# Layer norm blocks turned through three lent PSUM banks, later exponentials, and the memory's key sums on GpSimd

## The chip, the cores and the metric

The kernel runs on one core of one Trainium2 chip. Its engines are TensorE (PE, with its weight loads as PEld), VectorE (DVE), ScalarE (ACT), GpSimd (POOL) and SyncE (SP), which issues most DMAs. PSUM holds eight banks of 128 partitions by 512 fp32 values; TensorE writes there, ACT and DVE read it. The metric is the device time of one execution in microseconds (us), as the median of several runs; lower is better. Before the change the median of three runs is 2346.03 us (2342.25 to 2346.14).

## What is computed

A pre-norm transformer block on 2048 tokens of width 1024: layer norm, a memory-augmented attention of 32 heads of 32 (Infini-attention, four segments of 512 tokens), residual, a second layer norm, a GELU MLP of width 3584, residual. All in fp32. The part that the change touches is this, for each of the four segments `s`:

```python
phi = lambda t: jnp.where(t > 0, t + 1.0, jnp.exp(t))
logits = q_s @ k_s.T * scale + mask          # causal variant over the segment
a_dot  = softmax(logits) @ v_s
pq  = phi(q_s)
num = pq @ M                                  # memory of earlier segments
den = pq @ z + 1e-6                           # its key sums
o   = g * num / den + (1 - g) * a_dot
pk = phi(k_s)
M = M + pk.T @ v_s
z = z + pk.sum(over tokens)
```

`x` goes through `_layernorm` (mean and variance over the width, eps 1e-5) before the projections to q, k and v.

## The kernel before

Every fp32 matrix product is made of three passes in a rounded type: an operand is split into a high half (`yh`, `kh`, `pth`, ...: a cast, mostly on ACT) and a low half (`yl`, `kl`, `ptl`, ...: a subtraction, mostly on DVE), and `mm3` adds high by high, high by low and low by high in PSUM.

The tokens are worked in two halves of 1024, each of two segments (`sl` 0 and 1, so `s = 2 * half + sl`). A half has these stages: attention, output projection (`wo_first`, `wo_second`), second layer norm, the MLP's first product (class `Mixer`), and after the second half the MLP's second product (class `Second`) for all tokens.

**Attention.** The loop goes over eight groups `g` of four heads, inside it over the two segments. One pass is a unit, made by `dense(g, sl, ws, u)`: eight chunks of key projection into a bank `kps`, eight of query projection into `qps`, eight of value projection into `vps`, with a `yield` after each chunk. At each yield one of the six steps of a head of the unit before runs (`heads`, `slot`, the string `PLAN`): scores `pqk`, softmax (`pr`, `mx`, `nm`), transposes `ppt` of the probabilities with their halves `pth` and `ptl`, and products `po` with the values. 24 chunks of a unit thus lie beside the 24 steps of four heads.

After the keys are projected, `kh` (L408, ACT) and `kl` (L414, DVE) are the halves of `kps`; DMAs stack them into `ks`. `phi_parts` (L356) makes exp and relu of the same bank on ACT (`e` L358, `r` L359), named before `kl`; `phi_sum` (L364, DVE, two chunks later) adds them to `pk` and leaves the sum over the tokens in the column `zc`. With the queries it goes the same way: `qh` L422, `e`, `r`, `ql` L429, `pq`. Keys need phi in segments 0 to 2, queries in segments 1 to 3.

What is left of a unit (`late`, L461) runs inside the next one: value transposes `vn`, memory reads `pm` (`memory`, L472), the update `pmm` of the memory (`update`, L489) and the transposes `pom`. Their small matmuls are queued (`smalls`, `one_small`) and put singly between the transposes and products of the heads. The memory stands in `MZ`: for each group 128 columns of `M` (four blocks of 32 by 32 on the diagonal) and four columns of key sums. `update` writes the key sums: ACT spreads `zc` over four columns by the head mask `hsel`, into columns 128 to 131 of the bank of `pmm` (L491), and DVE adds them to `MZ` (L495), after four DVE adds of the blocks (L494). The next segment of the same group casts `MZ` to `mzh` (L441, DVE) and `mzl` (L442, POOL).

**PSUM.** The eight banks are named by tags: `d` has three (`ps_dense`: `kps`, `qps`, `vps`, `pkn`, `vn`, `pm`, `pmm`, `pom` in turn), `qk` two (`pqk`), `pt` two (`ppt`), `av` one (`po`). A tile takes a bank of its tag when the last reader of an earlier tile there is done.

**Layer norm before the projections.** `ln1(half, sl)` takes four tiles of 128 tokens: statistics on DVE, three small POOL instructions (L132, L133, L138) for scale `v` and offset `nb`, the scaling on ACT (`xt`, L167), then for each half of the width four transposes into one bank (L146, PE), the cast `yh` (L148, ACT) and the difference `yl` (L150, DVE). The bank comes from `take`: always the one of `av`. Segment 1 of each half is normalised inside the first unit of that half (`interleave(d, ln1(half, 1, ...))`), when no heads run yet; segment 0 of the second half inside the last nine pairs of the mixer's first half. Segment 0 of the first half has its own code (`opening`), which the change leaves alone.

**Order.** From the mixer to the end of a half, and in the opening, each engine keeps the order of the program (`in_order`). In the attention the framework's scheduler orders each engine's queue at build time, by program order and its own estimate of when inputs are ready; on the chip each queue then runs in that order.

Of the kernel before, what the change touches and what calls it, by code (L numbers as in the profile page):

```python
# [9 lines left out]
F32 = mybir.dt.float32  # L10
# [32 lines left out]
def build(tc, x, wq, wk, wv, wo, beta, w1, b1, w2, b2, out):  # L43
# [9 lines left out]
    ident = const.tile([P, P], F32, name="ident")  # L53
    make_identity(nc, ident)
    sel = const.tile([P, 76], F32, name="sel")
    hsel, gcol = sel[:, 0:4], sel[:, 8:8 + NG]
    nc.vector.memset(hsel, 0.0)
    for j in range(4):
        nc.vector.memset(hsel[32 * j:32 * j + 32, j:j + 1], 1.0)
    mhalf = const.tile([P, 1], F32, name="mhalf")  # L60
# [138 lines left out]
    def ln1(half, sl, delay=0, aside=None):  # L199
        xs = []  # L200
        for t in range(4):
            xt = lnp.tile([P, D], F32, tag="ln", name="xt", bufs=4)
            r0 = half * HT + (4 * sl + t) * P
            nc.sync.dma_start(xt, x[0, r0:r0 + P, :])
            xs.append(xt)
        for _ in range(delay):
            yield
        acts["y", sl] = yh, yl = seg_tiles(sl, "y")

        def take(name):  # L210
            return psum.tile([P, 512], F32, tag="av", name=name, bufs=1)

        yield from ln_tiles(lnp, xs, yh, yl, False, act=True, aside=aside,
                            fold=lambda src, t4: ln_transpose(lnp, src, yh, yl, t4, take))
# [125 lines left out]
    def attention(half, first):  # L340
# [15 lines left out]
        def phi_parts(ps):  # L356
            e, r = tmp("e"), tmp("r")
            nc.scalar.activation(e, ps, AF.Exp)  # L358
            nc.scalar.activation(r, ps, AF.Relu)  # L359
            return e, r  # L360
# [36 lines left out]
        def dense(g, sl, ws, u):  # L397
            s = 2 * half + sl
            behind = acts.pop("late", iter(()))
            kps = ws.pop("kps", None)  # L400
            if kps is None:
                kps = ps_dense("kps")
                for c in project(ws["k"], sl, "kps", kps):
                    if c >= 2:
                        next(behind, None)
                    yield
            kh, kl = tmpr("kh"), tmpr("kl")
            nc.scalar.copy(kh, kps)  # L408
            if s < 3:
                kparts = phi_parts(kps)  # L410
            qps = ps_dense("qps")
            for c in project(ws["q"], sl, "qps", qps):
                if c == 0:
                    nc.vector.tensor_tensor(kl, kps, raw(kh), op=ALU.subtract)  # L414
                    u["ks"] = stack(kh, kl, "ks", (0, 1, 0))
                if c == 2 and s < 3:
                    zc = ab.tile([P, 64], F32, name="zc", bufs=2)[:, 0:1]
                    pk = phi_sum(kparts, "pk", zc)
                next(behind, None)
                yield  # L420
            qh, ql = tmpr("qh"), tmpr("ql")
            nc.scalar.copy(qh, qps)  # L422
            if s > 0:
                qparts = phi_parts(qps)

            vps = ps_dense("vps")
            for c in project(ws["v"], sl, "vps", vps):
                if c == 0:
                    nc.vector.tensor_tensor(ql, qps, raw(qh), op=ALU.subtract)  # L429
                    u["qs"] = stack(qh, ql, "qs", (0, 0, 1))  # L430
                if s > 0:
                    if c == 2:
                        pq = phi_sum(qparts, "pq")
                    if c == 4:
                        while small:
                            one_small()
                        pqh, pql = tmpr("pqh"), tmpr("pql")
                        mzh = ab.tile([P, 256], F32R, name="mzh", bufs=1)[:, 0:132]
                        mzl = ab.tile([P, 256], F32R, name="mzl", bufs=1)[:, 0:132]
                        nc.scalar.copy(pqh, pq)  # L440
                        nc.vector.tensor_copy(mzh, MZ[:, g, :])  # L441
                        nc.gpsimd.tensor_tensor(mzl, MZ[:, g, :], raw(mzh), op=ALU.subtract)  # L442
                    if c == 5:
                        nc.gpsimd.tensor_tensor(pql, pq, raw(pqh), op=ALU.subtract)
                if c == 1 and s < 3:
                    pkn = ps_dense("pkn")
                    for i in range(4):
                        nc.tensor.transpose(pkn[:, i * P:(i + 1) * P], pk[:, i * P:(i + 1) * P], ident)
                    pkh, pkl = tmpr("pkh"), tmpr("pkl")
                    nc.scalar.copy(pkh, pkn)  # L450
                if c == 2 and s < 3:
                    nc.vector.tensor_tensor(pkl, pkn, raw(pkh), op=ALU.subtract)
                next(behind, None)
                yield
            vt = tmp("vt")
            nc.scalar.copy(vt, vps)
            vs = ab.tile([P, 16, 64], F32R, name="vs", bufs=2)
            u["vs"] = vs
            omt = u["omt"] = tmp("omt") if s > 0 else None

            def late():  # L461
                vn = ps_dense("vn")
                for c in range(4):
                    nc.tensor.transpose(vn[:, c * P:(c + 1) * P], vt[:, c * P:(c + 1) * P], ident)
                vn3 = vn.rearrange("p (a b) -> p a b", b=DH)
                nc.scalar.copy(vs[:, :, 0:32], vn3)
                nc.vector.tensor_tensor(vs[:, :, 32:64], vn3, raw(vs[:, :, 0:32]), op=ALU.subtract)
                yield
                if s > 0:
                    om = tmp("om")  # L470

                    def memory(i2, ps):  # L472
                        pm = ps.rearrange("p (a b) -> p a b", a=2)
                        rg = ab.tile([P, 2, 32], F32, name="rg", bufs=2)[:, :, 0:4]
                        nc.vector.tensor_scalar(rg, pm[:, :, 128:132], DEN_EPS, None, op0=ALU.add)
                        nc.vector.reciprocal(rg, rg)
                        nc.vector.tensor_tensor(
                            om[:, i2 * 256:(i2 + 1) * 256].rearrange("p (a h e) -> p a h e", a=2, h=4),
                            pm[:, :, 0:128].rearrange("p a (h e) -> p a h e", h=4),
                            rg.unsqueeze(3).to_broadcast([P, 2, 4, DH]), op=ALU.mult)  # L480

                    for i2 in range(2):
                        smalls("pm", [(lambda ps, ii=ii: ps[:, 256 * ii:256 * ii + 132],
                                       pqh[:, (2 * i2 + ii) * P:(2 * i2 + ii + 1) * P],
                                       pql[:, (2 * i2 + ii) * P:(2 * i2 + ii + 1) * P], mzh, mzl, True, True)
                                      for ii in range(2)], partial(memory, i2))
                left = len(small)
                if s < 3:
                    def update(pmm):  # L489
                        zs = pmm[:, P:P + 4]  # L490
                        nc.scalar.activation(zs, hsel, AF.Identity, scale=zc)  # L491
                        for j in range(4):
                            b = slice(32 * j, 32 * j + 32)
                            nc.vector.tensor_tensor(MZ[b, g, b], pmm[b, b], MZ[b, g, b], op=ALU.add)  # L494
                        nc.vector.tensor_tensor(MZ[:, g, 128:132], zs, MZ[:, g, 128:132], op=ALU.add)  # L495

                    smalls("pmm", [(lambda ps: ps[:, 0:P].rearrange("p (a b) -> p a b", a=4),
                                    pkh[:, c * P:(c + 1) * P], pkl[:, c * P:(c + 1) * P],
                                    vs[:, 4 * c:4 * c + 4, 0:32], vs[:, 4 * c:4 * c + 4, 32:64], c == 0, c == 3)
                                   for c in range(4)], update)  # L500
                total = len(small)
                while len(small) > total - left:
                    yield
                yield
                if s > 0:
                    pom = ps_dense("pom")
                    for i in range(4):
                        one_small()
                        nc.tensor.transpose(pom[:, i * P:(i + 1) * P], om[:, i * P:(i + 1) * P], ident)
                    nc.scalar.activation(omt, pom, AF.Identity, scale=gcol[:, g:g + 1])  # L510
                while small:
                    yield
            for _ in behind:
                one_small()
            acts["late"] = late()
# [890 lines left out]
```

## Time and profile before

| | |
|---|---|
| three runs | 2342.25, 2346.03, 2346.14 us |
| the profiled execution, its own time | 2343.49 us |
| its span, first to last instruction | 2341.4 us |
| mean granted TensorE clock | 0.998 |
| DVE busy | 1569.4 us (67%) in 3318 instructions |
| ACT busy | 1237.3 us (53%) in 2585 |
| POOL busy | 1019.0 us (44%) in 1005 |
| attention of the first and second half, with the first unit | about 23 to 540 us, about 909 to 1425 us |

"Idle before" and "waits" in the profile are time in which an engine had nothing running, put down to the instruction whose end let it go on. Of two engines that work beside each other only the one that the end of the program waits for counts. A matmul's duration overlaps that of the next: what counts for TensorE is the distance from one start to the next.

### The profile page before, as it was taken

The page shows a single profiled execution, that of the slowest core. Times are in us where ns is not written, and L with a number is a line of the kernel's source. Part 1 is how long each engine was busy: PE and PEld are TensorE (multiplying, and loading weights), DVE is VectorE, ACT ScalarE, POOL GpSimd, SP SyncE. Part 2 cuts the span into 40 slices and gives each one's busy share as a digit, 9 for nine tenths or more (in the row PEclk, how much of TensorE's full clock was granted, in tenths as well). Part 3 has the DMA queues.
Part 4 walks back from the last instruction along what each step waited for, and adds up shares of the span by engine and source line. Part 5 has one row for each costly group of instructions (what it writes and reads, how often), then busy time and mean ns, then how long its engine had stood idle before and what let it go on. Part 6 is the DMA issues. An engine that isn't in the chain of part 4 may idle for free.

```text
span 2341.4 us, 35348 instructions
## 1 busy us (share of the span) xinstructions
PE 2282.5 (97%) x11769; PEld 1889.6 (81%) x11769; DVE 1569.4 (67%) x3318; ACT 1237.3 (53%) x2585; POOL 1019.0 (44%) x1005
## 2 busy tenths in 40 slices
PE   7999999999999999999999999999999999999999
PEld 6888888878778887888888877778887878887887
DVE  6777777776665565777777777564566787568653
ACT  5777777785353445777777776363343233322321
POOL 4445454455104442555555545213444564155430
PEclk9999999999999999999999999999999999999999
DMA  5333333345366555433333334465567976577762
GB/s 172 96 89 91 88 83 85 90 109 185 124 209 176 180 157 145 114 88 84 84 86 87 85 100 147 143 207 174 168 189 245 352 246 195 170 237 230 248 220 93
DMA packets 322719, 355.36 MB, mean 152 GB/s; under 512 B 26190, under 2 KB 218730, under 8 KB 322538
## 3 DMA queue, kind: packets, MB, share of 16 engines
q1 hardware_dynamic: 259370, 316.40, 44.9%
q10 hardware_dynamic: 63168, 36.71, 5.2%
q8 instruction: 93, 1.52, 0.3%
q14 instruction: 88, 0.72, 0.1%
HBM read 226.59 MB, written 76.09 MB: 129 GB/s over the span
## 4 chain that ended last, share of the span: by engine, by line
PE 71%; DVE 10%; ACT 7%; DMA 4%; issue 3%; POOL 3%; SPq 1%; ACTq 0%; POOLq 0%; DVEq 0%
PE po L1243 20%; PE bps L861 8%; PE dps L861 5%; PE ppt L560 5%; PE po L580 4%; PE cps L861 4%; PE pqk L528 3%; PE kps L118 2%; PE kps L120 2%; PE kps L119 2%; PE vps L118 2%; PE vps L119 2%; PE vps L120 2%; ACT pr L537 1%; PE qps L118 1%
## 5 line engine op out<-in xcount | busy, mean ns | idle before, releaser
L544 POOL TENSOR_SCALAR pr<-pr,nm,gate 128x128 f32<-128x128 f32 (+3 forms) x512 | 326.4, 648 | 380.4 <-DVE nm L541 306.8
L537 ACT ACTIVATE pr<-pr,mx 128x256 f32<-128x256 f32 (+3 forms) x512 | 287.7, 562 | 171.8 <-DVE mx L529 170.2
L567 DVE TENSOR_TENSOR ptl<-ppt,pth 128x512 fp32r<-128x512 f32 (+1 forms) x384 | 227.5, 598 | 63.9 <-ACT pth L562 61.3
L529 DVE CUSTOM_DVE_ANT_0 pr<-pqk,mask 128x256 f32<-128x256 f32 (+3 forms) x512 | 243.6, 483 | 36.7 <-PE pqk L528 35.0
L560 PE MATMUL ppt<-ident,pr 128*128 128x128 f32 x1280 | 222.5, 277 | 1.2 <-DVE ptl L567 1.2
L562 ACT CAST pth<-ppt 128x512 fp32r<-128x512 f32 (+1 forms) x384 | 194.1, 518 | 33.7 <-PE ppt L560 28.3
L1253 DVE TENSOR_TENSOR c<-c,po 128x512 f32<-128x512 f32 x160 | 105.3, 682 | 148.1 <-PE po L1243 148.1
L560 PEld LDWEIGHTS ppt<-ident,pr 128*128 128x128 f32 x1280 | 164.3, 140 | 30.7 <-DVE ptl L567 2.4
L95 POOL TENSOR_TENSOR wl<-wr,wh 128x1024 fp32r<-128x1024 f32 x53 | 126.9, 2395 | 86.4 <-ACT wh L94 30.8
L528 PE MATMUL pqk<-ks,qs 96*128 96x256 f32 (+3 forms) x512 | 162.8, 319 | 1.7 <-DVE mx L529 1.7
L580 PE MATMUL po<-ptl,vs 128*64 128x512 f32 (+3 forms) x512 | 154.2, 311 | 3.3 <-DVE ptl L567 2.3
L580 PE MATMUL po<-pth,vs 128*64 128x512 f32 (+3 forms) x512 | 155.6, 326 | 1.8 <-ACT pth L562 1.5
L976 POOL TENSOR_TENSOR s<-r 128x512 f32<-128x512 f32 x28 | 43.5, 1554 | 234.9 <-DVE sa L992 112.9
L1243 PE MATMUL po<-w2h,zh 128*128 128x512 f32 x378 | 120.8, 389 | 0.0
L528 PEld LDWEIGHTS pqk<-ks,qs 96*128 96x128 f32 x512 | 96.0, 188 | 26.8 <-DVE mx L529 7.1
L541 DVE RECIPROCAL nm<-mx 128x2 f32<-128x2 f32 x256 | 42.4, 165 | 110.0 <-ACT pr L537 109.7
L1113 POOL TENSOR_TENSOR w2r<-w2r 128x512 f32<-128x512 f32 x54 | 89.8, 1679 | 56.0 <-DMA w2r<-in_B_w 33.6
L861 PE MATMUL bps<-zh,sa 128*128 128x512 f32 x336 | 110.7, 390 | 1.6 <-DVE u L1006 1.6
L861 PE MATMUL bps<-zh,sb 128*128 128x512 f32 x336 | 111.1, 391 | 1.1 <-DVE u L1018 1.1
L118 PE MATMUL kps<-yh,wh 128*128 128x512 f32 (+1 forms) x264 | 109.8, 416 | 0.6 <-ACT yh L148 0.6
L118 PE MATMUL vps<-yh,wh 128*128 128x512 f32 x256 | 108.9, 425 | 0.4 <-ACT omt L510 0.4
L118 PE MATMUL qps<-yh,wh 128*128 128x512 f32 x256 | 106.3, 415 | 0.0
(238 smaller groups left out, 6692.3 us busy)
## 6 DMA issues: line engine op xcount, KB each, us to landing
hr<-h_dram SPq DMA_DIRECT2D x112, 448.0 KB, 4.8
w2r<-in_B_w SPq DMA_DIRECT2D x122, 256.0 KB, 4.3
r<-in_B_w SPq DMA_DIRECT2D x56, 512.0 KB, 4.5
h_dram<-ht ACTq DMA_DIRECT2D x84, 256.0 KB, 3.9
ks<-kh SPq DMA_DIRECT2D x256, 64.0 KB, 2.0
qs<-qh SPq DMA_DIRECT2D x256, 64.0 KB, 2.0
wr<-in_A_wo SPq DMA_DIRECT2D x32, 512.0 KB, 3.9
wx<-in_B_w SPq DMA_DIRECT2D x56, 256.0 KB, 3.9
```

The source lines that it names most:

```text
L95: getattr(nc, lo_eng).tensor_tensor(lo, w, raw(hi), op=ALU.subtract)
L118: nc.tensor.matmul(ps, ah, bh, start=first, stop=False)
L528: nc.tensor.matmul(pqk[:, :n], u["qs"][j][:, i * P:(i + 1) * P], u["ks"][j][:, 0:n], start=True, stop=True)
L529: nc.vector.tensor_tensor_reduce(out=st["pr"][:, offs[i]:offs[i] + n], in0=pqk[:, :n], in1=mask[:, 512 - n:512], op0=ALU.add, op1=ALU.min, ...
L537: nc.scalar.activation(pi, pi, AF.Exp, bias=mx[:, i:i + 1], scale=-1.0, accum_out=mx[:, 4 + i:5 + i])
L544: nc.gpsimd.tensor_scalar(pi, pi, nm[:, 4 + k:5 + k], gate[:, 1, 4 * g + j:4 * g + j + 1], op0=ALU.mult, op1=ALU.mult)
L560: nc.tensor.transpose(ppt[:, o:o + P], pr[:, offs[i] + jk * P:offs[i] + (jk + 1) * P], ident)
L562: nc.scalar.copy(pth[:, base:base + w], ppt[:, :w])
L567: nc.vector.tensor_tensor(o, x0, x1, op=ALU.subtract)
L580: nc.tensor.matmul(po[:, P * jk:], v, st[part][:, koff[jk]:koff[jk] + w], start=(jk, part) == (0, "pth"), stop=(jk, part) == (2, "ptl"))
L861: nc.tensor.matmul(ps, x_[:, c, :], y_[:, c, :], start=first and c == 0 and n == 0, stop=last and c == 3 and n == 2, skip_group_check=True)
L1243: nc.tensor.matmul(ps, x_[:, k], y_[k], start=opens and k == 0 and i == 0, stop=closes and k == self.KP - 1 and i == 2, skip_group_check=True)
```

## The change

Three edits.

1. `ln1`'s `take` goes round through three banks: for segment 1 the two of `pt` and the one of `av`, for segment 0 (only the second half uses it) the two of `qk` and the one of `av`.
2. `phi_parts` of the keys, and that of the queries, is named inside the first chunk of the next projection, after `kl` (`ql`) and the stacking DMAs, instead of right after `kh` (`qh`).
3. The key sums leave `update`. A new column per group, `zcol` in the tile `sel`, zeroed once, is kept by GpSimd: at the seventh chunk of the value projection (`c == 6`) POOL adds `zc` to it and writes `hsel` times it into the four columns of `MZ`. The ACT instruction of L491 and the DVE instruction of L495 are gone.

```diff
-    hsel, gcol = sel[:, 0:4], sel[:, 8:8 + NG]
+    hsel, gcol, zcol = sel[:, 0:4], sel[:, 8:8 + NG], sel[:, 16:16 + NG]
     nc.vector.memset(hsel, 0.0)
+    nc.vector.memset(zcol, 0.0)
...
+        homes = [("pt", 2), ("pt", 2), ("av", 1)] if sl else [("qk", 2), ("qk", 2), ("av", 1)]
+
         def take(name):
-            return psum.tile([P, 512], F32, tag="av", name=name, bufs=1)
+            homes.append(homes.pop(0))
+            return bank(name, *homes[-1])
...
             nc.scalar.copy(kh, kps)
-            if s < 3:
-                kparts = phi_parts(kps)
             qps = ps_dense("qps")
             for c in project(ws["q"], sl, "qps", qps):
                 if c == 0:
                     nc.vector.tensor_tensor(kl, kps, raw(kh), op=ALU.subtract)
                     u["ks"] = stack(kh, kl, "ks", (0, 1, 0))
+                    if s < 3:
+                        kparts = phi_parts(kps)
...
             nc.scalar.copy(qh, qps)
-            if s > 0:
-                qparts = phi_parts(qps)
...
                     nc.vector.tensor_tensor(ql, qps, raw(qh), op=ALU.subtract)
                     u["qs"] = stack(qh, ql, "qs", (0, 0, 1))
+                    if s > 0:
+                        qparts = phi_parts(qps)
...
+                if c == 6 and s < 3:
+                    nc.gpsimd.tensor_scalar(zcol[:, g:g + 1], zcol[:, g:g + 1], zc, None, op0=ALU.add)
+                    nc.gpsimd.tensor_scalar(MZ[:, g, 128:132], hsel, zcol[:, g:g + 1], None, op0=ALU.mult)
...
                     def update(pmm):
-                        zs = pmm[:, P:P + 4]
-                        nc.scalar.activation(zs, hsel, AF.Identity, scale=zc)
                         for j in range(4):
                             b = slice(32 * j, 32 * j + 32)
                             nc.vector.tensor_tensor(MZ[b, g, b], pmm[b, b], MZ[b, g, b], op=ALU.add)
-                        nc.vector.tensor_tensor(MZ[:, g, 128:132], zs, MZ[:, g, 128:132], op=ALU.add)
```

`bank(name, tag, bufs)` returns `psum.tile([P, 512], F32, tag=tag, name=name, bufs=bufs)`.

## The prediction

> **What bounds the kernel now.** First the page: who is busy, and which engine carries the chain that ends last.
>
> ```profile
> span 2341.4 us, 35348 instructions
> PE 2282.5 (97%) x11769; PEld 1889.6 (81%) x11769; DVE 1569.4 (67%) x3318; ACT 1237.3 (53%) x2585; POOL 1019.0 (44%) x1005
> PE 71%; DVE 10%; ACT 7%; DMA 4%; issue 3%; POOL 3%; SPq 1%; ACTq 0%; POOLq 0%; DVEq 0%
> ```
>
> TensorE is busy for all but 59 us of the span. The change touches no matmul, so it can only win back waits of TensorE, and work taken from ACT or DVE counts only where TensorE waits for it. Next the busy time by stretches of 60 us: a steady stretch of each half's attention, and the second MLP product.
>
> ```profile
> 240.00:300.00 60.00, 59.02 (x360) 49.43 (x360) 44.49 (x140) 43.65 (x113) 29.26 (x36) 1.00 0.35 89
> 1080.00:1140.00 60.00, 59.51 (x363) 50.19 (x364) 44.37 (x142) 43.15 (x111) 30.37 (x40) 1.00 0.33 84
> 1980.00:2040.00 60.00, 60.00 (x267) 49.69 (x266) 32.17 (x36) 16.56 (x22) 12.70 (x8) 1.00 0.49 147
> ```
>
> The columns are PE, PEld, DVE, ACT, POOL, granted clock, DMA share and GB/s. The clock is full. In attention TensorE lacks 1.0 us (first half) or 0.5 us (second) in 60, so little can be won; ACT, DVE and POOL have 15 us and more free in each. Now the waits of TensorE by name: the whole span first, then the second half's steady attention (950 to 1379 us, three rows), then the first half's (60 to 500 us, two rows).
>
> ```profile
> PE pmm L390 <- DVE kl L414: 7.0, 8, 1.1
> PE pt L146 <- DVE yl L150: 3.5, 3, 1.2
> PE pt L146 <- ACT xt L167: 1.9, 1, 1.9
> PE kps L118 <- ACT yh L148: 0.6, 2, 0.4
> ...
> PE pqk L528 <- DVE mx L529: 1.4, 7, 0.2
> PE po L580 <- DVE ptl L567: 1.3, 6, 0.2
> PE pom L509 <- DVE om L477: 0.8, 5, 0.2
> ...
> PE pmm L390 <- DVE kl L414: 5.9, 7, 0.8
> PE po L580 <- DVE ptl L567: 1.0, 4, 0.5
> ```
>
> (Total us, times, longest.) The first two rows are the change's targets: the update `pmm` waits for a bank until `kl` has read the keys out of it, and layer norm's transposes wait for their one bank until `yl` has.
>
> **Edit 1, three banks.** In the first unit one half tile goes round like this (TensorE, ACT, DVE, TensorE):
>
> ```profile
> 34.16 0.66 PE L146 MATMUL pt<-ident,xt 128*128 128x128 f32 x4 [1.15 <-DVE yl L150]
> 34.86 0.59 ACT L148 CAST yh<-pt 128x512 fp32r<-128x512 f32 x1
> 35.48 0.69 DVE L150 TENSOR_TENSOR yl<-pt,yh 128x512 fp32r<-128x512 f32 x1 [0.77 <-ACT yh L148]
> 36.27 0.60 PE L146 MATMUL pt<-ident,xt 128*128 128x128 f32 x4
> 31.67 1.24 ACT L167 ACTIVATE xt<-xt,nb,v 128x1024 f32<-128x1024 f32 x1 [1.26 <-POOL nb L138]
> 45.20 0.63 PE L146 MATMUL pt<-ident,xt 128*128 128x128 f32 x4
> ```
>
> One bank gives a half tile per 36.27 - 34.16 = 2.11 us; eight of them run to the last at 45.20. Three banks allow one per 0.70 us, and then the cast (0.59) and the inputs set the pace: the last `xt` ends at 31.67 + 1.24 = 32.91, two transposes, casts and a difference behind it take 0.66 + 2 x 0.59 + 0.69 = 2.5, so all is normalised by about 35.5. TensorE has the first unit's own products until about 40 now, and without the waits until about 37. So the three waits for `yl` (3.5) and the 0.4 for `yh` at the next unit's keys can go: 3.9 us at most. What is late next is `xt` itself, whose fourth tile waits for POOL. How the queue of TensorE is then laid out I can't read; where a transpose stands too early the wait is for `xt`, and the second half's first unit has such a one, 1.9 us. Bounds: 0 to 3.9. I take **3.0**, nearer the upper end, since two of the four inputs are ready before their bank now. In the second half's first unit no wait for `yl` stands in the list, only 0.2 of the 0.6 for `yh`; the 1.9 for `xt` is before any bank is short. I take 0. Segment 0 of the second half lies in mixer pairs, where the transposes wait for nothing: 0; its new banks (`qk`) are not used by the pairs (`d` and `pt`).
>
> **Edit 2, the exponentials.** The bank of `kps` in a unit of segment 0, in order ACT, DVE, TensorE:
>
> ```profile
> 81.31 0.59 ACT L408 CAST kh<-kps 128x512 fp32r<-128x512 f32 x1 [1.14 <-PE kps L120]
> 81.79 0.51 ACT L537 ACTIVATE pr<-pr,mx 128x256 f32<-128x256 f32 x1
> ...
> 82.68 0.58 ACT L358 ACTIVATE e<-kps 128x512 f32<-128x512 f32 x1
> 83.16 0.59 ACT L359 ACTIVATE r<-kps 128x512 f32<-128x512 f32 x1
> ...
> 82.81 0.17 DVE L541 RECIPROCAL nm<-mx 128x2 f32<-128x2 f32 x1 [1.01 <-ACT pr L537]
> 83.78 0.69 DVE L414 TENSOR_TENSOR kl<-kps,kh 128x512 fp32r<-128x512 f32 x1 [0.80 <-ACT r L359]
> ...
> 84.52 0.33 PE L390 MATMUL pmm<-vs,pkh 128*128 128x128 f32 x1 [0.84 <-DVE kl L414]
> ```
>
> `kl` needs only `kh`, done at 81.90, but starts 0.03 us behind `r`: the accesses of ACT and DVE to one bank are kept apart, reads too, and `r` was named first. Then `pmm` starts 0.05 us after `kl`, with TensorE idle for 0.84. With `kl` named first: DVE is idle from 82.81 - 1.01 = 81.80, so `kl` runs 81.9 to 82.6, beside the two softmax exponentials that ACT does anyway until 82.68; `e` and `r` stay where they are, and the bank is free at `r`'s end, 83.75, instead of 84.47: **0.72 us earlier**. Seven units of the first half have this: 7 x 0.72 = **5.0 us**. The eighth wait lies in segment 3, whose keys have no exponentials, so it stays (1.1, the longest in its row). If DVE took `kl` only after the reciprocal at 82.81 the release would be at 82.98 + 0.69 + 2 x 0.5 = 84.7, and 7 x 0.2 = 1.6 us would be lost. Bounds: -5.9 (the row of the first half goes whole) to +1.6.
>
> [...]
>
> DVE's own waits shrink too:
>
> ```profile
> DVE kl L414 <- ACT r L359: 18.1, 22, 1.8
> DVE ql L429 <- ACT r L359: 8.1, 22, 0.6
> DVE MZ L494 <- ACT pmm L491: 10.8, 15, 0.9
> ```
>
> Behind `kl` and `ql` in DVE's queue stand the score reductions `mx`, `ptl` and `om`, for which TensorE waits in the small rows above: 1.4 + 1.3 + 0.8 in the second half, 1.0 in the first, 4.5 us. DVE reaches them up to 18.1 / 22 = 0.8 us earlier at the keys and 8.1 / 22 = 0.4 at the queries, while each of these waits is 0.2 to 0.5, so they could all go. But ACT now has the wait that DVE had: `e` and `r` stand behind `kl` or `ql`, and behind them in ACT's queue the exponentials `pr` and the casts `pth`, for which `ptl` waits. I take half, **2.3 us**; bounds 0 to 4.5, with the loss below as a rival.
>
> **Edit 3, the key sums.** Removed and, as the nearest rows to what is added, POOL's instructions on a column:
>
> ```profile
> L491 ACT ACTIVATE pmm<-sel,zc x24: 247/261/272, 59.5 to 1386.1; 128x4 f32<-128x4 f32 x24
> L495 DVE TENSOR_TENSOR MZ<-pmm,MZ x24: 161/162/164, 60.6 to 1387.2; 128x4 f32<-128x4 f32 x24
> L132 POOL TENSOR_SCALAR v<-mv x32: 192/192/1055, 6.2 to 1521.1; 128x1 f32<-128x1 f32 x32
> L138 POOL TENSOR_SCALAR nb<-mv,v x31: 266/267/1303, 7.1 to 1522.8; 128x1 f32<-128x1 f32 x31
> ```
>
> ACT loses 24 x 0.26 = 6.3 us, DVE 24 x 0.16 = 3.9 and its 10.8 of waiting. None of it stands directly before TensorE; what it brings is `ptl` sooner, in the 2.3 already. POOL gets 48 instructions of 0.19 to 0.27: 9 to 13 us, hidden in the half of its time that is free. `zc` was written twelve chunks before, and the write to `MZ` waits at most for the cast `mzh` two chunks before, which POOL's own `mzl` awaited already; so no wait is new. Queued behind are the normalisations of `pr`, 0.5 us later once in a unit; transposes of them wait for `ptl`, never for POOL. I take 0; bounds 0 to 24 x 0.5 = 12 us, if every pair delayed TensorE.
>
> The pair can also hold up DVE: a sum of two SBUF operands takes twice its 0.68 us beside a POOL subtraction.
>
> ```profile
> 53.34 1.33 DVE L364 SCALAR_TENSOR_TENSOR pk<-e,r 128x512 f32<-128x512 f32 x1
> 51.72 2.38 POOL L95 TENSOR_TENSOR wl<-wr,wh 128x1024 fp32r<-128x1024 f32 x1 [2.92 <-PE pqk L528]
> ```
>
> [...]
>
> **The sum.** 3.0 + 5.0 + 2.3 + 0 = 10.3 us. The profiled execution took 2343.49, so 2333.2. The median, 2346.03, lies 2.5 above that execution; I place the forecast between 2333.2 and 2346.03 - 10.3 = 2335.7, at **2334 us**.
>
> **Rivals.**
> (a) *The bank comes free no earlier*: ACT fills the time in front of `e` with other work, or DVE is late with `kl`, so `r` ends near 84.5 again. For it: the same four readings one behind the other. Against it: ACT has two exponentials in hand just while `kl` would run, and DVE is idle then. Only the layer norm and a little remain: about 4 us, 2342 (bounds -1.6 to the 1.6 loss around it: 2339 to 2346).
> (b) *The transposes wait for `xt` instead of the bank*: the 1.9 row shows such a wait, against it stands that the inputs come every 1.2 to 2.5 us, ahead of their use. Without the 3.0: 2337.
> (c) *Slower: ACT stands still behind `ql`.* With the queries it is tighter:
>
> ```profile
> 63.29 0.67 DVE L591 TENSOR_TENSOR ot<-po,ot 32x512 f32<-32x512 f32 x1
> ...
> 62.93 0.59 ACT L422 CAST qh<-qps 128x512 fp32r<-128x512 f32 x1
> 63.41 0.60 ACT L358 ACTIVATE e<-qps 128x512 f32<-128x512 f32 x1
> ```
>
> `qh` ends at 63.52, DVE is free at 63.96, and `ql`, as long as `kl`, would end at 64.65. If `e` keeps its place in ACT's queue, it starts 64.65 - 63.41 = 1.2 us later, and behind it the last exponential `pr`, `pth`, `ptl` and TensorE's products `po`, which wait already. The point from which it decides is the order in that queue, `e` ahead of `pr`: then the 24 query units lose 24 x (1.2 - 0.4 that `ql` gains) = 19 us, and 2334 + 19 = 2353. Against it: at 81.79 the queue put exponentials that were ready ahead of `e`.
> (d) *Nothing moves*: the order of the queues comes out such that each gain is given back: 2346.
>
> **Chances.** Forecast 0.52, (a) 0.23, (b) 0.10, (c) 0.09, (d) 0.06. 0.2% is 4.7 us, about what a measurement of this kernel tells from no change: the bound of faster is 2341.3. The forecast and (b) are faster, and of (a) 0.09 more: 0.71. Same: 0.14 of (a), 0.06 of (d), a little of (c): 0.21. Slower: 0.08. Range: downward all of `pmm`'s removable waits, 5.5 more of layer norm and small rows, but hardly all together: 2328; upward through (a) and (d): 2346.
>
> **What would show it.** Right: `kl` and `ql` start at the end of `kh` and `qh` without a wait for `r`; the wait of `pmm` falls from 0.84 us to between 0.1 and 0.3, released by `r`; the row of `pt` on `yl` is gone and layer norm's last transposes in the first unit come before 37 us; `pqk`, `po` and `pom` wait for less. Wrong: ACT idle in front of `e` for `kl` or `ql`, new waits of `po` for `pth`, `pt` waiting for `xt`, or a wait of TensorE for POOL's `pr`.

## The result, and the profile after

| | before | after |
|---|---|---|
| median of six runs (before: the three above and three more) | 2344.78 us | 2328.94 us |
| lowest to highest | 2340.09 to 2346.14 | 2327.21 to 2330.70 |
| the profiled execution, its span | 2341.4 us | 2325.4 us |

The ratio is 0.9937 [0.9925, 0.9949]: 0.6% faster, 15.8 us by the medians. The forecast was 2334.

First the page of the changed kernel: span and busy time.

```profile
span 2325.4 us, 35324 instructions
PE 2279.2 (98%) x11769; PEld 1891.8 (81%) x11769; DVE 1566.8 (67%) x3295; ACT 1232.5 (53%) x2561; POOL 1021.0 (44%) x1053
```

TensorE runs the same 11769 matmuls. The three other engines changed by 2 to 5 us of busy time. Of the 16.0 us of span 12.7 are idle time of TensorE (58.9 before, 46.2 after); the other 3.3 are a shorter recorded busy time for the same matmuls. So the waits come next, those of TensorE by name, from 22 to 60 us, from 72 to 500 us (first half) and from 960 to 1370 us (second half). Columns: total us, times, longest.

```profile
PE ppt L564 <- DVE ptl L571: 0.4, 1, 0.4
...
PE po L584 <- DVE ptl L571: 1.7, 6, 0.3
PE po L584 <- ACT pth L566: 1.1, 1, 1.1
...
PE po L584 <- DVE ptl L571: 2.4, 7, 0.3
PE pmm L394 <- DVE kl L416: 1.1, 1, 1.1
```

`pt` on `yl` (3.5) is gone, and so are seven of the eight waits of `pmm` (the one of segment 3 stays), `pqk` on `mx` and `pom` on `om`. `po` on `ptl` has grown, from 0.5 to 1.7 in the first half and from 1.3 to 2.4 in the second: the next thing that is late. The one wait of `po` on `pth` (1.1) is not new: before it stands at 508.9 us, behind the end of this window.

The first unit, as busy time in two stretches (columns PE, PEld, DVE, ACT, POOL, clock, DMA share, GB/s), before:

```profile
22.00:60.00 38.00, 33.95 (x192) 27.49 (x191) 21.91 (x59) 23.26 (x54) 15.74 (x25) 1.00 0.45 121
60.00:73.00 13.00, 12.32 (x69) 9.70 (x68) 11.46 (x33) 10.76 (x26) 9.12 (x11) 1.00 0.65 189
```

and after:

```profile
22.00:60.00 38.00, 37.41 (x211) 30.72 (x210) 27.81 (x71) 27.93 (x63) 21.21 (x33) 1.00 0.53 148
60.00:73.00 13.00, 13.00 (x80) 10.95 (x79) 10.33 (x31) 10.60 (x28) 8.28 (x10) 1.00 0.53 140
```

The last group of layer norm's transposes there, in the timeline of after (start, us, engine, line):

```profile
36.85 0.60 PE L147 MATMUL pt<-ident,xt 128*128 128x128 f32 x4
```

In the same 51 us TensorE is busy 4.1 us longer and issues 30 matmuls more; the transposes end at 37 instead of 45 us.

The bank of the keys in segment 0, after (ACT, DVE, TensorE):

```profile
75.33 0.59 ACT L412 CAST kh<-kps 128x512 fp32r<-128x512 f32 x1 [1.14 <-PE kps L121]
75.81 0.51 ACT L541 ACTIVATE pr<-pr,mx 128x256 f32<-128x256 f32 x1
...
76.70 0.58 ACT L362 ACTIVATE e<-kps 128x512 f32<-128x512 f32 x1
77.18 0.59 ACT L363 ACTIVATE r<-kps 128x512 f32<-128x512 f32 x1
...
75.95 0.69 DVE L416 TENSOR_TENSOR kl<-kps,kh 128x512 fp32r<-128x512 f32 x1
...
77.80 0.91 DVE L368 SCALAR_TENSOR_TENSOR pk<-e,r 128x512 f32<-128x512 f32 x1 [0.80 <-ACT r L363]
...
77.82 0.33 PE L394 MATMUL pmm<-vs,pkh 128*128 128x128 f32 x1
```

`kl` starts 0.03 us behind `kh`, beside ACT's two softmax exponentials; `e` and `r` keep their distance to `kh` (1.37 and 1.85 us, as before), and `pmm` starts 0.05 behind `r`'s end at 77.77, where it started behind `kl`. But DVE now stands 0.80 us for `r` in front of `pk`: its wait has moved, not gone. DVE's waits for `r` over the whole run, after (before: `kl` 18.1, `ql` 8.1):

```profile
DVE pk L368 <- ACT r L363: 20.5, 23, 1.7
...
DVE pq L368 <- ACT r L363: 2.8, 9, 0.5
```

### The profile page after: what moved, and what is told of

Its sections match the earlier page's. It is cut to its first block, busy times and chain, and to the rows that moved or that the text cites. A ratio compares the mean times of both kernels' runs of the same rounds, so it can differ in the third digit from the quotient of the medians.

```text
span 2325.4 us, 35324 instructions
## 1 busy us (share of the span) xinstructions
PE 2279.2 (98%) x11769; PEld 1891.8 (81%) x11769; DVE 1566.8 (67%) x3295; ACT 1232.5 (53%) x2561; POOL 1021.0 (44%) x1053
## 4 chain that ended last, share of the span: by engine, by line
PE 75%; DVE 9%; ACT 7%; issue 3%; DMA 3%; POOL 2%; SPq 0%; ACTq 0%; POOLq 0%; DVEq 0%
PE po L1247 22%; PE bps L865 8%; PE dps L865 5%; PE ppt L564 5%; PE po L584 5%; PE cps L865 3%; PE vps L120 2%; PE vps L119 2%; PE vps L121 2%; PE pqk L532 2%; PE kps L119 2%; PE kps L121 2%; PE kps L120 2%; ACT pr L541 2%; DVE ptl L571 2%
## 5 line engine op out<-in xcount | busy, mean ns | idle before, releaser
L548 POOL TENSOR_SCALAR pr<-pr,nm,gate 128x128 f32<-128x128 f32 (+3 forms) x512 | 320.2, 635 | 360.5 <-DVE nm L545 272.2
L1247 PE MATMUL po<-w2h,hl 128*128 128x512 f32 x322 | 102.9, 389 | 1.5 <-DVE c L1257 1.5
```

The source lines that it names most:

```text
L548: nc.gpsimd.tensor_scalar(pi, pi, nm[:, 4 + k:5 + k], gate[:, 1, 4 * g + j:4 * g + j + 1], op0=ALU.mult, op1=ALU.mult)
L1247: nc.tensor.matmul(ps, x_[:, k], y_[k], start=opens and k == 0 and i == 0, stop=closes and k == self.KP - 1 and i == 2, skip_group_check=True)
```

## The experiments

All are compared with the kernel before on the same chip. "After" below is the changed kernel. The second table is worked out from the traces: the time between the starts of two named TensorE instructions, less the same in the trace of before. Units 0-1 run from the first `qps` product to the last `vps` product of the second unit, the steady attention from there to the last `vps` of the half's last unit but one, its tail from there to the middle of the output projection; units 16-17 run from the second half's first `kps` product to the last `vps` product of its second unit.

| run | median us | ratio to before |
|---|---|---|
| e1_banks | 2335.57 | 0.9967 [0.9955, 0.9979] |
| e2_exps | 2339.82 | 0.9984 [0.9974, 0.9995] |
| e3_sums | 2345.09 | 1.0009 [0.9996, 1.0021] |
| all_again | 2329.09 | 0.9940 [0.9925, 0.9954] |
| no_sums | 2332.93 | 0.9956 [0.9943, 0.9969] |
| no_exps | 2337.72 | 0.9975 [0.9967, 0.9984] |
| k_only | 2338.31 | 0.9980 [0.9971, 0.9990] |
| q_only | 2329.48 | 0.9943 [0.9930, 0.9956] |
| keys_half0 | 2326.58 | 0.9940 [0.9926, 0.9953] |
| sums_dve | 2332.89 | 0.9961 [0.9949, 0.9974] |
| pool_more | 2359.39 | 1.0076 [1.0063, 1.0089] |
| v_on_dve | 2322.80 | 0.9921 [0.9906, 0.9936] |

| us against before | units 0-1 | steady, half 0 | units 16-17 | steady, half 1 |
|---|---|---|---|---|
| time before | 47.98 | 410.51 | 57.06 | 408.35 |
| after | -5.11 | -3.34 | +1.81 | -4.04 |
| all_again | -5.08 | -3.17 | +1.93 | -3.95 |
| e1_banks | -5.32 | +0.11 | -0.41 | +0.10 |
| e2_exps | +0.80 | +0.77 | +1.79 | -4.01 |
| e3_sums | +1.63 | +1.09 | +0.60 | +0.01 |
| no_sums | -5.13 | +0.79 | -0.41 | -4.07 |
| no_exps | -4.89 | +1.17 | +1.91 | +0.02 |
| k_only | -5.05 | -2.67 | +1.86 | +1.62 |
| q_only | -4.95 | +0.61 | +0.23 | -5.78 |
| keys_half0 | -5.13 | -3.41 | +1.83 | -5.73 |
| sums_dve | -5.15 | +0.11 | +1.74 | -4.14 |
| pool_more | -3.54 | +18.87 | +0.27 | -2.15 |
| v_on_dve | -5.15 | -3.32 | -0.63 | -5.69 |

The steady columns repeat to 0.2 us in the two traces of the changed kernel. The rest of the program, which no edit touches, differs by up to 7 us from one execution to the next: in the second MLP product, from 1500 us on, TensorE waited 8.1 us for `c` in the trace of before and 4.8 in that of after. That is why stages are compared here, and whole times by medians only.

**Each edit alone, and all again.**

e1_banks:
```diff
-            return psum.tile([P, 512], F32, tag="av", name=name, bufs=1)
+            homes.append(homes.pop(0))
+            return bank(name, *homes[-1])
```


> Edit 1 alone. My theory: the first unit's transposes no longer wait for yl, so the first unit with its follower ends 4 to 5 us earlier (the changed kernel's trace: 5.1 from the first query matmul to the end of the second unit's values, with the edits together), the wait of pmm for kl stays at 0.84 us seven times, and the second half's first unit loses up to 2 us, since there transposes now stand in front of other matmuls: 2341 to 2343 us where before is 2345. Rival: the gain of the first unit comes from kl standing ahead of the exponentials (edit 2), then edit 1 alone gives under 2 us.

e2_exps (the same for `qparts`, behind `ql`):
```diff
-            if s < 3:
-                kparts = phi_parts(kps)
...
                     u["ks"] = stack(kh, kl, "ks", (0, 1, 0))
+                    if s < 3:
+                        kparts = phi_parts(kps)
```


> Edit 2 alone. My theory: pmm's wait falls from 0.84 to 0.11 us seven times, released by r, and the waits of pqk and pom go; the steady attention of both halves gains 0.5 and 0.6 us per group as in the changed kernel, 7 to 8 us in all, layer norm's waits for yl stay (3.5): about 2337 us. Rival: the steady gain needs DVE's relief by edit 3 (its wait for the spread of the key sums, 10.8 us in all), then edit 2 alone gives the 5 us of pmm in the first half and nothing in the second.

e3_sums:
```diff
+                if c == 6 and s < 3:
+                    nc.gpsimd.tensor_scalar(zcol[:, g:g + 1], zcol[:, g:g + 1], zc, None, op0=ALU.add)
+                    nc.gpsimd.tensor_scalar(MZ[:, g, 128:132], hsel, zcol[:, g:g + 1], None, op0=ALU.mult)
...
-                        nc.scalar.activation(zs, hsel, AF.Identity, scale=zc)
...
-                        nc.vector.tensor_tensor(MZ[:, g, 128:132], zs, MZ[:, g, 128:132], op=ALU.add)
```


> Edit 3 alone. My theory: no wait of TensorE ends on what it removes, so within 1 us of before, 2344 to 2346, with POOL some 10 us busier. Rival: DVE comes to ptl, om and the scores sooner, and the small waits of the second half (3.5 us) go with this edit alone: 2341.

all_again is the changed kernel a second time.


> The changed kernel again, for its scatter and for the stages that no edit touches. In its trace the stages from the second half's output projection to the end came out 4.1 us shorter than before's, and the opening 0.9. My theory: those are waits for DMAs that vary from one execution to the next (before has one of 2.1 us at 2156 us, after a DMA that was late), so a second trace of each kernel differs there by several us; the attention stages repeat to 0.3 us. Rival: the shift of the attention against the DMAs does it, and the 4.1 us come again.

Edit 1 is worth 5.1 to 5.3 us in the first two units, the same in each kernel that has it, and nothing in the steady attention. By the whole times e1_banks gains more than that, 8.6 us, and lies 5 us below what was expected; by its trace the rest lies in stages that it doesn't touch. Edit 3 alone can't be told from no change by the whole time. By stages it costs 1.1 us of steady attention in the first half, and so it does with edit 1 beside it (no_exps, below: +1.17). `ppt`, of which before had no wait in that stretch, now waits for `ptl` there (e3_sums, 72 to 500 us):

```profile
PE ppt L561 <- DVE ptl L568: 0.9, 6, 0.2
```

e2_exps and e3_sums are the two traces in which TensorE's clock is at half for 3.4 us from 44 us on, so their numbers for units 0-1 (+0.80, +1.63) hold that as well. all_again repeats the steady stages to 0.2 us; its stages behind the second attention came out 5.3 us shorter than before's, again, as the rival had it. But in e3_sums, whose attention is 3 us longer than before's, these stages came out 5.9 shorter, and in v_on_dve, whose attention is 16 us shorter, 0.3 longer. So the shift of the attention is not what does it.

Edit 2 alone brings its 4.0 us in the second half, but in the first, where seven waits of 0.84 us were to go, nothing. The waits of TensorE in e2_exps, 72 to 500 us, say where they went:

```profile
PE po L580 <- DVE ptl L567: 6.4, 13, 0.7
```

`pmm` is down to 0.11 us each, and `po`, some 8 us behind it, waits. Neither the theory nor the rival put the gain in the second half alone.

**Two edits at a time.** no_sums is after without edit 3, no_exps after without edit 2; their diffs are those above.


> Edits 1 and 2 without 3: the key sums stay on ACT and DVE. After the first runs my theory is that edit 3, worth nothing by itself, is what lets edit 2's gain stand in the first half: with edit 2 alone the update's wait fell as reckoned, but po waits for ptl 13 times, 6.4 us, and the first half's steady attention lost 0.8 us instead of gaining 3.3. So here the first half's steady attention is 0.5 to 1.0 us longer than before's and po waits 6 us there, the second half's gains 4.0: 2333 us, 4 above the changed kernel. Rival: the waits of po come from the layer norm that edit 2 alone leaves as it was, then they are gone here and the time is the changed kernel's, 2329.

> Edits 1 and 3 without 2: the exponentials stay ahead of kl and ql. My theory: first unit 5 us better, the seven waits of pmm at 0.84 us stay, steady attention as before within 1 us in both halves, and in the second half's first unit TensorE doesn't go slowly after its wait for xt: 2336 to 2338 us. Rival: with the layer norm out of the way edit 3 brings the small waits of the second half down by itself: 2333.

no_sums has the same 6.4 us of `po` on `ptl`; after, with edit 3 on top, has 1.7. So edit 3, which alone costs 1.1 us of the steady first half, is worth 4.1 us of steady attention (+0.79 to -3.34) once edit 2 is there. The place in no_sums (ACT, DVE, TensorE):

```profile
83.73 0.26 ACT L494 ACTIVATE pmm<-sel,zc 128x4 f32<-128x4 f32 x1
83.92 0.85 ACT L565 CAST pth<-ppt 128x512 fp32r<-128x512 f32 x2
...
84.02 0.79 DVE L497 TENSOR_TENSOR MZ<-pmm,MZ 32x32 f32<-32x32 f32 x4 [0.70 <-ACT pmm L494]
84.82 0.16 DVE L498 TENSOR_TENSOR MZ<-pmm,MZ 128x4 f32<-128x4 f32 x1
84.90 1.01 DVE L570 TENSOR_TENSOR ptl<-ppt,pth 128x512 fp32r<-128x512 f32 x2
...
85.63 0.39 PE L583 MATMUL po<-ptl,vs 128*64 128x384 f32 x1 [0.69 <-DVE ptl L570]
```

DVE stands 0.70 us for ACT's spread of the sums, then adds, and only then makes `ptl`. Before, TensorE came here 0.72 us later, since it had waited at `pmm`. In after the same stretch reads:

```profile
83.55 0.77 DVE L499 TENSOR_TENSOR MZ<-pmm,MZ 32x32 f32<-32x32 f32 x4
84.65 1.02 DVE L571 TENSOR_TENSOR ptl<-ppt,pth 128x512 fp32r<-128x512 f32 x2 [0.34 <-ACT pth L566]
```

The additions begin without a wait, DVE is ready 0.34 us ahead of `pth`, and `po` waits 0.11.

**Keys and queries apart.** k_only is after with the queries' exponentials in the old place, q_only after with the keys' in the old place:
```diff
             nc.scalar.copy(qh, qps)
+            if s > 0:
+                qparts = phi_parts(qps)
...
                     u["qs"] = stack(qh, ql, "qs", (0, 0, 1))
-                    if s > 0:
-                        qparts = phi_parts(qps)
```


> The changed kernel with the exponentials of the queries back in their old place, those of the keys a chunk later. My theory: pmm's waits are at 0.11 us as in the changed kernel (they hang on the keys), pom's waits of the second half go too, but pqk and po of the second half wait as before (0.2 us each, 7 times each): first half's steady attention 3 us better than before's, second half's 1 to 2: 2331 us. Rival: all of the second half's gain comes from the keys: 2329, or less than the changed kernel, if the queries' order costs po its remaining waits.

> The changed kernel with the exponentials of the keys back in their old place, those of the queries a chunk later. My theory: pmm waits 0.84 us seven times as before, and the second half gains from pqk and po, 2 to 3 us: 2334 us. Rival: the queries' order alone costs ACT its place ahead of po and the first half gets slower than before's by some 3 us: 2338.

Beside no_exps the keys bring 3.8 us in the first half and cost 1.6 in the second; the queries bring 0.6 and 5.8. Both expectations missed: k_only came out 7 us slower than expected, in part since the keys alone lose in the second half, and q_only 4.5 us faster. The waits of TensorE in the steady second half (955 to 1355 us), k_only first, then q_only:

```profile
PE po L584 <- DVE ptl L571: 3.6, 13, 0.3
PE pqk L532 <- DVE mx L533: 1.2, 6, 0.2
```
```profile
PE pom L513 <- DVE om L484: 0.6, 4, 0.2
```

What the queries' edit does there is seen in the order of ACT's and DVE's queues, with the old place (no_exps):

```profile
980.02 0.59 ACT L426 CAST qh<-qps 128x512 fp32r<-128x512 f32 x1
980.50 0.61 ACT L362 ACTIVATE e<-qps 128x512 f32<-128x512 f32 x1
980.99 0.72 ACT L541 ACTIVATE pr<-pr,mx 128x512 f32<-128x512 f32 x1
...
981.70 0.60 ACT L363 ACTIVATE r<-qps 128x512 f32<-128x512 f32 x1
982.18 0.60 ACT L566 CAST pth<-ppt 128x512 fp32r<-128x512 f32 x1
...
982.33 0.69 DVE L433 TENSOR_TENSOR ql<-qps,qh 128x512 fp32r<-128x512 f32 x1 [0.32 <-ACT r L363]
982.94 0.68 DVE L571 TENSOR_TENSOR ptl<-ppt,pth 128x512 fp32r<-128x512 f32 x1
```

and with the new one (q_only):

```profile
975.91 0.58 ACT L426 CAST qh<-qps 128x512 fp32r<-128x512 f32 x1
976.40 0.73 ACT L541 ACTIVATE pr<-pr,mx 128x512 f32<-128x512 f32 x1
...
977.11 0.58 ACT L566 CAST pth<-ppt 128x512 fp32r<-128x512 f32 x1
977.58 0.61 ACT L362 ACTIVATE e<-qps 128x512 f32<-128x512 f32 x1
...
976.60 0.67 DVE L431 TENSOR_TENSOR ql<-qps,qh 128x512 fp32r<-128x512 f32 x1
...
977.72 0.69 DVE L571 TENSOR_TENSOR ptl<-ppt,pth 128x512 fp32r<-128x512 f32 x1 [0.31 <-ACT pth L566]
```

`pr` and `pth` now come ahead of `e` and `r`, and `ql` ahead of the wait: `ptl` starts 1.8 us behind `qh` instead of 2.9.

**Keys only where they pay.** keys_half0:
```diff
             nc.scalar.copy(kh, kps)
+            if s == 2:
+                kparts = phi_parts(kps)
...
-                    if s < 3:
+                    if s < 2:
                         kparts = phi_parts(kps)
```


> The changed kernel with one thing undone: in the second half (segment 2) the keys' exponentials are named where they were before, in the first half and for the queries a chunk later. Theory (the terms add: in the steady attention of the first half the keys are worth -3.8 us and the queries -0.6, in the second the keys cost +1.7 and the queries bring -5.8): the first half stays at -3.2 against the kernel before, the second comes to -5.8 instead of -4.0, about 2327 us in all, 1.7 below the changed kernel; the wait of po for ptl in the second half (7 of 0.34 us) is gone. Rival (the second half's 1.7 us come from how the queues happen to lie and not from the keys' place): no better than the changed kernel, 2329.

2326.58 us, and -3.41 and -5.73 in the two halves: the terms add as the theory said, and `po` on `ptl` is gone from the second half. By the whole time alone the two can't be told apart: the ratio is 0.9940, after's 0.9937.

**What of edit 3 matters.** sums_dve:
```diff
-                if c == 6 and s < 3:
-                    nc.gpsimd.tensor_scalar(zcol[:, g:g + 1], ...
-                    nc.gpsimd.tensor_scalar(MZ[:, g, 128:132], ...
...
                             nc.vector.tensor_tensor(MZ[b, g, b], pmm[b, b], MZ[b, g, b], op=ALU.add)
+                        nc.vector.tensor_scalar(zcol[:, g:g + 1], zcol[:, g:g + 1], zc, None, op0=ALU.add)
+                        nc.vector.tensor_scalar(MZ[:, g, 128:132], hsel, zcol[:, g:g + 1], None, op0=ALU.mult)
```


> The changed kernel with the two instructions for the key sums on VectorE instead of GpSimd; ScalarE's spread stays out. Theory (without edit 3 the last ptl of a unit is late because VectorE stands still for ScalarE's spread, 0.70 us, and ScalarE does it before pth): the steady attention of the first half keeps its -3.2 us, 2329 in all, though VectorE has one instruction more than with edits 1 and 2 alone; po does not wait for ptl. Rival (what counts is VectorE's own time in front of ptl, 0.16 us of one addition and now two small instructions): the first half goes back to +0.8 as with edits 1 and 2 alone, 2333, with 13 waits of po for ptl.

The theory missed: the time, 2332.89, is the rival's. But the waits are neither's: five of 0.91 us and one of 0.34, where none or thirteen were expected. At the place shown above the wait of `po` fell as the theory had it, from 0.69 to 0.11 us. The new ones stand in the other units (DVE, then POOL):

```profile
115.21 1.36 DVE L498 TENSOR_SCALAR MZ<-sel 128x4 f32<-128x4 f32 x1
...
116.56 0.99 DVE L570 TENSOR_TENSOR ptl<-ppt,pth 128x512 fp32r<-128x512 f32 x2
...
115.26 1.28 POOL L597 TENSOR_TENSOR ot<-ot,omt 128x512 f32<-128x512 f32 x1 [0.97 <-DVE ot L594]
```

and as waits of TensorE from 72 to 500 us:

```profile
PE po L583 <- DVE ptl L570: 4.9, 6, 0.9
```

A write of 128x4 that took 0.23 us elsewhere in this trace takes 1.36 beside an addition on POOL: it starts 0.05 us ahead of the addition and ends 0.03 behind its end (116.57 and 116.54). What ties the two together was not shown. The same pair of instructions stands before each of the five waits of 0.91. Before the sixth, 0.34, they start together as well (304.76 and 304.81), and the write takes 0.23. So ACT's spread is what edit 3 has to remove, but GpSimd as the new home counts too: with the pair on DVE, behind GpSimd's own additions, 3.5 of the 4.1 us are given back (+0.11 to -3.34).

**How much room GpSimd has.** pool_more:
```diff
-                    nc.gpsimd.tensor_scalar(MZ[:, g, 128:132], hsel, zcol[:, g:g + 1], None, op0=ALU.mult)
+                    for _ in range(9):
+                        nc.gpsimd.tensor_scalar(MZ[:, g, 128:132], hsel, zcol[:, g:g + 1], None, op0=ALU.mult)
```


> The changed kernel with GpSimd's second instruction of the pair, the write of the sums into MZ, repeated eight times more (the same values again): 24 x 8 x 0.27 = 52 us more on GpSimd. Theory (the pair is hidden in GpSimd's free time, 0.2 to 0.3 us per instruction): eight more delay the normalisations of pr by 2.2 us once a unit, which the transposes do not wait for; within 1 us of the changed kernel, 2328 to 2331, and no wait of TensorE for pr. Rival (the pair delays the softmax and was paid for): 24 x 2.2 = 52 us at most, 2335 to 2380, with new waits of ppt for GpSimd's pr or of DVE beside it.

The theory missed: 2359.39, 30 us over after, 22 of them in the steady first half. POOL and TensorE at one place:

```profile
115.32 3.40 POOL L452 TENSOR_SCALAR MZ<-sel 128x4 f32<-128x4 f32 x9
...
119.94 2.37 POOL L549 TENSOR_SCALAR pr<-pr,nm,gate 128x384 f32<-128x384 f32 x4
...
120.65 0.43 PE L565 MATMUL ppt<-ident,pr 128*128 128x128 f32 x1 [1.66 <-POOL pr L549]
```

and the waits from 60 to 500 us:

```profile
PE ppt L565 <- POOL pr L549: 13.5, 14, 1.7
```

Nine writes take 3.40 us, eight of them 3.1 more than one; 1.66 of it comes out as a wait. So in after POOL stands, by this difference, about 1.4 us ahead of the transposes in these units, with the one pair of edit 3 (0.7 us) already in. Of the 22 us some 12 are longer waits; five stretches of 3.4 us at half clock behind such waits, about 1.7 us lost in each, make up most of the rest (the mean granted clock from 100 to 500 us is 0.98, in after 1.00). In the unit of the other segment, where the writes stood at 80.88, no wait followed. Half of GpSimd's time is free, but not here.

**The first unit of the second half.** In after its two units take 1.8 us longer than before, though edit 1's banks cost nothing in e1_banks, where up to 2 us had been expected. TensorE's wait for `xt` there is much the same, 1.87 us in after, 1.89 in before and in e1_banks; what differs is the pace behind it. Seven traces have TensorE at half clock for 3.4 us there (the last section; its products of 512 columns then start 0.43 us apart instead of 0.23), and they are the seven with +1.74 to +1.93 in the table (no_exps, for which it was not expected, among them); the others lie between -0.63 and +0.60. Half the pace for 3.4 us is a loss of 1.7. v_on_dve is keys_half0 with one weight split moved:
```diff
-                ws[n] = load_block(wp, w, g * P, 3, "vector" if g or n == "k" else "scalar")
+                ws[n] = load_block(wp, w, g * P, 3, "vector" if g or n == "k" else "scalar",
+                                   "vector" if half and not g and n == "v" else "gpsimd")
```


> keys_half0 with one thing more: for the first unit of the second half the low part of the weights v is computed by VectorE instead of GpSimd, so that GpSimd reaches layer norm's v and nb about 1 us sooner. Theory (TensorE's wait for xt there hangs on GpSimd's weight split of 2.4 us just before v and nb): the wait falls from 1.9 us to about 0.9; and if TensorE's half pace after it follows from the length of the idle time, it goes too, so that the two units take 1 to 3 us less than in keys_half0, 2324 to 2326 in all. Rival (the wait then goes to VectorE, whose statistics for xt stand behind the split of 1.4 us; or the half pace is a matter of phase alone): no difference, or up to 1.4 us more.

The wait falls to 0.93 and a second one of 0.33, and the two units take 2.5 us less than in keys_half0: 0.6 of shorter waits, the rest pace. At 2322.80 us, 0.9921 [0.9906, 0.9936], it has the lowest median of all; its interval overlaps that of after.

## Why the prediction was right, and where not

- **The whole.** 2334 was forecast with 10.3 us of gain; 15.8 were measured, 12 to 17.6 by the interval, so the direction was right and the size some 5 us short. By stages after gains 5.1 + 3.3 + 4.0 us, 1.5 more in the two tails of attention, and loses 1.8: 12.1. The remainder lies in stages that no edit touches, almost all of it (4.1) behind the second attention, where the traces of all kernels lie anywhere between 5.9 us below before's and 1.0 above. That edits 2 and 3 together were forecast at 5.0 + 2.3 = 7.3 us, and the two steady stretches gave 3.3 + 4.0, is luck: with edit 3, which the sum put at 0, left out, they give 3.3 (no_sums).
- **Edit 1, 3.0, bound 3.9: mis-sized; 5.1.** The waits that went were counted, but not `po`'s, 0.67 us (0.15 and 0.53) at 65 to 67 us, and not that an idle gap costs more than it shows: from start to start TensorE lost 0.16 us on top at 30.05 (1.08 of gap, 1.24 lost), and at `pmm` 0.26 (0.84 and 1.10). One new wait came, `ppt` on `ptl`, 0.4. No transpose waits for `xt` that did not before: rival (b) is out.
- **Edit 2, the bank of `pmm`, 5.0: right in mechanism and size at its place**, 0.72 us seven times (start to start, 1.10 lost each before, 0.38 after). Wrong was to book it as final. Alone it was given back at `po` (+0.8 in the first half), as rival (d) has it. Rival (a) is out: the readings still follow one another (`kl` ends at 76.64, `e` starts at 76.70, and in the traces of before and after no reading of `kps` or `qps` by DVE overlaps one by ACT), but `kl` now has its turn while ACT works elsewhere.
- **Small waits, 2.3.** For the queries more: 5.8 us in the second half, through `pqk` and `po`. For the keys less than nothing there, 1.6 to 1.7 lost. The step that failed is "DVE reaches them up to 18.1 / 22 = 0.8 us earlier at the keys": there DVE's 18.1 us of waiting for `r` moved from `kl` to `pk` (20.5 after), and `pk` stands ahead of the reductions just as `kl` had. At the queries the wait on `r` did shrink (8.1 to 2.8, at `pq`).
- **Edit 3, 0: wrong as a term of a sum.** Alone it is 0 by the whole time, as said, and costs 1.1 us by stages; behind edit 2 it is worth 4.1 us, because ACT's spread was what came late next. I had noted DVE's 10.8 us of waiting there and put its end into the 2.3. POOL's pair takes 0.29 and 0.30 us, 14 us in all, a little over the 9 to 13 reckoned. That the transposes of `pr` wait for `ptl`, "never for POOL", is wrong as well: with about 1.4 us more on POOL they do.
- **Rival (c), ACT standing behind `ql`**, did not come: the queue put `pr` and `pth` ahead of `e`, so that `ql` was done in the meantime. That was the point named to decide it. At the keys the sign did come: ACT stands in front of `e` for `kl` eight times in after, 3.3 us in all, once in each unit of segment 1 of the first half. The six waits of `po` for `ptl` that are left in the first half, 0.27 to 0.28 us each, stand in six of the same units some 7 us later; in q_only, without the keys' edit, neither is there to that length (`po` twice, 0.15). That the one causes the other was not tested.

## What to carry over

A wait of the bounding engine that is removed is worth its length only if the next item on that engine's path has as much room; look up that item's slack, and price two edits together where one makes room and the other uses it. An instruction that waits in an in-order queue can pass its wait on when the order changes, as `kl` passed it to `pk` (18.1 us of waits for `r` at `kl` before, 20.5 at `pk` after); ask who stands in it now and who is queued behind. A free half of an engine's time says nothing about the microsecond in front of a consumer: read the slack at the place.

## What the runs showed of the hardware

TensorE's clock fell to half (0.50) after waits of 1.89 us and less, in some traces and not in others with the same wait. After (columns as above, PEclk the third from the end), then the wait itself:

```profile
906.20:908.30 2.10, 2.10 (x10) 2.00 (x11) 0.38 (x1) 2.02 (x3) 1.70 (x5) 0.57 0.98 345
908.30:909.70 1.40, 1.40 (x5) 1.11 (x4) 1.40 (x3) 1.40 (x3) 1.01 (x3) 0.50 0.35 119
```

```profile
906.20 1.74 PE L147 MATMUL pt<-ident,xt 128*128 128x128 f32 x8 [1.87 <-ACT xt L168]
```

and q_only:

```profile
909.90:911.60 1.70, 1.70 (x11) 1.35 (x9) 0.83 (x2) 1.70 (x4) 1.34 (x5) 1.00 0.89 319
```

```profile
909.04 1.09 PE L147 MATMUL pt<-ident,xt 128*128 128x128 f32 x8 [1.87 <-ACT xt L168]
```

Of the 13 traces with this wait of 1.87 to 1.89 us seven show the half clock behind it, six don't; it lasts 3.4 us, in sums_dve it begins about 1 us later behind the wait than in after (1.3 and 0.3 us), and in pool_more it follows five of six waits of 1.65 to 1.67 us. The clock records of the traces tell them apart. In before and after all changes of the clock lie whole multiples of 3.41 us apart, some of them hundreds of us: counted in 3.413 us, the second and third start of the half clock lie 77 and 233 behind the first in before, 260 and 416 in after. If this grid is laid over TensorE's idle times, the falls of the clock within the program follow stretches of the grid with 1.87 and 2.52 us of idle time in before, 1.87 and 2.79 in after. The seven traces with the half clock have the whole wait in one stretch; in the six others it goes over the border of two, with 1.15 to 1.77 us in the fuller one (before: 0.51 and 1.37). No sharp bound shows between: the clock also fell after 1.51 (e3_sums) and stayed after 1.67 (before, the stretch at 2152.6 us) and 1.88 (e3_sums, at 1806 us). So with the same wait it is the phase against this grid that goes with the half clock, by the records of 13 traces; no run moved the phase alone. v_on_dve shortened the wait to 0.93, and the half clock was gone.
